# A two-layer recurrent-memory transformer block on one core: order plan iterated backward and forward, softmax over all rows from partition 0, V strips on ScalarE, V weights loaded first

## The chip, the core and the metric

One core of a Trainium2 chip runs the whole program. Its engines are TensorE (PE in the rows, PEld its weight loads), VectorE (DVE), ScalarE (ACT), GpSimd (POOL) and SyncE (SP), which here issues the transfers. The metric is the device time of one execution in microseconds (us).

## What is computed

The input x has 2048 rows of 512. Two layers follow, each with the same weights: memory-augmented recurrent attention A, then a gated FFN B.

```python
x = x + _A_ref(_layernorm(x), mem0, Wq, Wk, Wv, Wo, seg_len=32)   # 32 heads of 128
x = x + _B_ref(_layernorm(x), w_gate, w_up, w_down)               # 512 -> 1792 -> 512
x = x + _A_ref(_layernorm(x), mem0, Wq, Wk, Wv, Wo, seg_len=32)
x = x + _B_ref(_layernorm(x), w_gate, w_up, w_down)
...
for s in range(n_seg):                       # 64 segments, one after the other
    h = concatenate([mem, xs])               # 8 memory rows + 32 rows of the segment
    q, k, v = h Wq, h Wk, h Wv
    p = softmax(where(mask, q k^T * scale, -1e9))
    o = (p v) Wo
    mem = o[:, :8]; outs.append(o[:, 8:])
```

The memory of one segment is an output of the segment before it, so the 64 segments of a layer are a chain.

## The kernel before

The program runs 70 steps. Step t works on segment t of the first layer (j = 0) and segment t − 6 of the second (j = 1) at once: 40 rows each, 80 columns in one matmul. Steps 0 to 5 have the first layer alone, steps 64 to 69 the second. `hT` holds the transposed rows of a step; its memory columns come from the step before (L679, L684), and that is the recurrence.

`emit_step` goes through the 32 heads in groups of six (the last has two). For a group: Q and K matmuls (L577), casts to `qku` (L807, on ScalarE), scores (L596), the softmax on VectorE (mask add `st` L606, once for each layer; maximum L611; subtraction L613; exponential on ScalarE L616; sum L618; reciprocal L620; product `pb` L625, once for each layer), a transpose by matmul (L636), a cast to `ptsb`, probabilities times V (L649), a cast to `otsb`, and the output matmuls (L666). The first layer's scores lie in partitions 0 to 63, the second's in 64 to 103, so that one instruction can serve both where they need the same.

V rows come in two ways. The 24 last rows of each segment (`XS`) are computed by blocks of four segments (`v_pass`, L458), cast to `vst` and written to scratch memory `scr`, from which each step loads its rows into `vsb`. The memory rows and the rest change with every step: `strips` (L553) computes 32 rows for all heads, and eight casts put them into `vsb` (32 partitions x 512 each). Casts given as `("ACT", "DVE")` go to whichever engine the planner finds free; L807 is such a cast on ScalarE, L809 on VectorE.

The FFN of a block of four segments (`ffn`, L730 up and gate, L749 down, weights streamed from memory) and the V passes are background work for TensorE between the attention matmuls.

No loop sets the order on the engines. `Planner` collects tasks with an engine, an assumed duration, dependences and buffers, and `plan` makes a list schedule: a task's priority is the length of the longest chain behind it (`tail`), plus a `boost`. What it yields is emitted in that order, and each engine executes its instructions in order.

Of the kernel before, what the change touches and what calls it, by code (L numbers as in the profile page):

```python
# [10 lines left out]
F32 = mybir.dt.float32  # L11
# [63 lines left out]
class Planner:  # L75
# [48 lines left out]
    def plan(self):  # L124
# [4 lines left out]
        for bf in self.bufs:  # L129
# [118 lines left out]
class Kern:  # L248
# [48 lines left out]
    def setup_tiles(self):  # L297
# [11 lines left out]
        self.maskb = c.tile([P, L], F32, name="maskb")  # L309
        self.negh = c.tile([P, 1], F32, name="negh")  # L310
# [29 lines left out]
        self.bank = Pool([pp.tile([P, 512], F32, name=f"bank{i}") for i in range(8)], {"bg": 3, "v": 2})  # L340
        self.qkp = Pool(self.qku)
        self.vstp = Pool(self.vst)
        self.xnp = Pool(self.xn)

    def setup_consts(self):
# [15 lines left out]
        nc.vector.memset(self.negh[:], -0.5)  # L361
        for t_ in self.hT:
# [7 lines left out]
    def load_weights(self):  # L370
# [37 lines left out]
    def layernorm_T(self, xb, xkey):  # L408
# [11 lines left out]
        pl.add("ACT", act_ns(D) + 180, lambda: nc.scalar.activation(out=xn[:, :], in_=xb, func=ACTF.Identity, bias=ln[:, 10:11], scale=ln[:, 9:10]),  # L420
# [28 lines left out]
    def v_pass(self, tile, keys, pieces):  # L449

        nc, pl, DC = self.nc, self.pl, self.DC
        for k in range(self.H // 4):
# [8 lines left out]
            vs = pl.buf(self.vstp)  # L461
# [405 lines left out]
```

## Time and profile before

| | |
|---|---|
| median of 3 runs | 2171.83 us (2168.66 to 2173.26) |
| the profiled execution | 2167.7 us, its span 2165.9 us |
| granted TensorE clock, mean | 0.978 of full speed |
| busy: PE, PEld, DVE, ACT | 1890.6, 1595.0, 1521.9, 1318.9 us |
| instructions | 94004 |

Busy times are unions of the records of an engine; those of matmuls overlap, and a busy TensorE is not one at its peak. The chain that ended last is followed back from the last instruction to whatever released it.

### The profile page before, as it was taken

To read this page: it belongs to the slowest core of one execution; us is meant where nothing else is said; L and a number is where in the kernel's file an instruction comes from. 1 tells how busy PE (TensorE), PEld (TensorE's weight loads), DVE (VectorE), ACT (ScalarE), POOL (GpSimd) and SP (SyncE) were. 2 spreads that over 40 slices of the span, in tenths; PEclk is the share of its full clock that TensorE was granted. 3 is DMA by queue.
4 is the path that set the end of the run, shared out by engine and by line. 5 is a ranking of instruction groups with operands and counts; after the bars stand their busy time and mean duration, and the time that the engine had idled before them with its cause. 6 is when DMAs were issued, how large, how long until landed. Compare 5 with 4: busy or idle time off the path is not lost.

```text
span 2165.9 us, 94004 instructions
## 1 busy us (share of the span) xinstructions
PE 1890.6 (87%) x40901; PEld 1595.0 (74%) x41116; DVE 1521.9 (70%) x4377; ACT 1318.9 (61%) x2949; POOL 50.0 (2%) x93
## 2 busy tenths in 40 slices
PE   3798888989889898988989899898889899898886
PEld 2576677878777776877778787787778777777775
DVE  4475777777777775777777777767777777777664
ACT  2465666566666664666665666666665666666554
POOL 1000000000000000000000000000000000000000
PEclk8999999999999999999999999999999999999999
DMA  9314132533425245342525334252515244252633
GB/s 323 115 47 141 50 102 59 167 92 119 130 80 173 57 130 162 107 133 85 157 58 168 95 116 128 80 165 85 159 54 170 81 121 126 79 164 76 168 88 107
DMA packets 363808, 255.43 MB, mean 118 GB/s; under 512 B 21626, under 2 KB 349058, under 8 KB 363394
## 3 DMA queue, kind: packets, MB, share of 16 engines
q1 hardware_dynamic: 363394, 249.40, 38.9%
q8 instruction: 322, 5.28, 1.0%
q14 instruction: 92, 0.75, 0.1%
HBM read 222.04 MB, written 27.26 MB: 115 GB/s over the span
## 4 chain that ended last, share of the span: by engine, by line
DVE 44%; PE 36%; ACT 7%; issue 5%; DMA 4%; SPq 1%; DVEq 0%; ACTq 0%; POOLq 0%; POOL 0%
PE bank L577 13%; DVE st L606 10%; DVE pb L625 8%; PE bank L666 8%; DVE vsb L809 7%; PE bank L730 5%; DVE st L613 4%; DVE mx L611 4%; PE bank L458 4%; DVE sm L618 4%; ACT vsb L807 3%; DMA scr<-vst 2%; DVE hff L737 2%; PE bank L649 2%; PE bank L749 2%
## 5 line engine op out<-in xcount | busy, mean ns | idle before, releaser
L577 PE MATMUL bank<-hT,wq_sb 128*128 128x80 bf16 (+1 forms) x8960 | 628.2, 199 | 13.2 <-DVE hT L679 6.2
L577 PE MATMUL bank<-hT,wk_sb 128*128 128x80 bf16 (+1 forms) x8960 | 627.9, 199 | 2.9 <-issue 1.6
L807 ACT CAST qku<-bank 128x480 bf16<-128x480 f32 (+3 forms) x770 | 394.6, 514 | 192.4 <-PE bank L577 176.8
L577 PEld LDWEIGHTS <-wq_sb 128*128 128x128 bf16 x8960 | 459.1, 100 | 57.5 <-issue 47.4
L577 PEld LDWEIGHTS <-wk_sb 128*128 128x128 bf16 x8960 | 454.7, 100 | 2.7 <-DMA wk_sb<-in_A_Wk_dram 1.4
L606 DVE TENSOR_TENSOR st<-bank,maskb 64x240 f32<-64x240 f32 (+3 forms) x768 | 288.7, 376 | 216.3 <-PE bank L596 200.2
L666 PE MATMUL bank<-otsb,wo_sb 128*128 128x80 bf16 (+1 forms) x8960 | 379.1, 199 | 23.2 <-ACT otsb L807 21.7
L666 PEld LDWEIGHTS <-wo_sb 128*128 128x128 bf16 x8960 | 349.9, 100 | 44.6 <-issue 28.2
L625 DVE TENSOR_TENSOR pb<-st,rs 64x240 bf16<-64x240 f32 (+3 forms) x768 | 286.4, 373 | 17.1
L616 ACT ACTIVATE st<-st 104x240 f32<-104x240 f32 (+5 forms) x420 | 159.9, 381 | 191.8 <-DVE st L613 187.9
L807 ACT CAST otsb<-bank 128x480 bf16<-128x480 f32 (+3 forms) x420 | 200.9, 485 | 100.4 <-PE bank L649 93.6
L809 DVE CAST vsb<-bank 32x512 bf16<-32x512 f32 x262 | 180.0, 687 | 75.9 <-ACT vsb L807 71.2
L807 ACT CAST vsb<-bank 32x512 bf16<-32x512 f32 x298 | 172.0, 577 | 94.3 <-DVE vsb L809 85.2
L636 PE MATMUL bank<-ident,pb 128*128 128x80 bf16 (+1 forms) x2240 | 148.5, 200 | 79.6 <-DVE pb L625 65.7
L807 ACT CAST ptsb<-bank 128x480 bf16<-128x480 f32 (+3 forms) x348 | 169.9, 503 | 73.9 <-PE bank L636 72.4
L596 PE MATMUL bank<-qku 128*128 128x80 bf16 (+1 forms) x2240 | 169.7, 199 | 49.6 <-ACT qku L807 46.1
L636 PEld LDWEIGHTS <-pb 128*128 128x128 bf16 x2240 | 106.2, 100 | 117.5 <-DVE pb L625 92.7
L649 PE MATMUL bank<-ptsb,vsb 128*128 128x80 bf16 (+1 forms) x2240 | 147.0, 200 | 49.5 <-ACT ptsb L807 18.4
L618 DVE TENSOR_REDUCE sm<-st 104x6 f32<-104x240 f32 (+5 forms) x420 | 155.2, 369 | 44.6 <-ACT st L616 41.1
L730 PE MATMUL bank<-xnT,wg 128*128 128x128 bf16 x1792 | 179.1, 224 | 5.6 <-DVE vsb L809 1.5
L730 PE MATMUL bank<-xnT,wu 128*128 128x128 bf16 x1792 | 178.9, 224 | 3.8 <-DMA wu<-in_B_w_up_dram 3.7
L596 PEld LDWEIGHTS <-qku 128*128 128x128 bf16 x2240 | 116.4, 99 | 74.4 <-ACT qku L807 56.6
(69 smaller groups left out, 2085.0 us busy)
## 6 DMA issues: line engine op xcount, KB each, us to landing
wg<-in_B_w_gate_dram SPq DMA_DIRECT2D x224, 256.0 KB
wu<-in_B_w_up_dram SPq DMA_DIRECT2D x224, 256.0 KB
wd<-in_B_w_down_dram SPq DMA_DIRECT2D x224, 256.0 KB
vsb<-scr SPq DMA_DIRECT2D x512, 48.0 KB
scr<-vst SPq DMA_DIRECT2D x176, 96.0 KB
scr<-vst SPq DMA_DIRECT2D x144, 32.0 KB
wv_sb<-in_A_Wv_dram SPq DMA_DIRECT2D x4, 1024.0 KB
wq_sb<-in_A_Wq_dram SPq DMA_DIRECT2D x5, 768.0 KB
```

Source lines behind the costliest of these rows:

```text
L577: nc.tensor.matmul(o_ap, lhsT=W[:, c, h * P:(h + 1) * P], rhs=mv(c), start=(c == 0), stop=(c == DC - 1))
L596: nc.tensor.matmul(s_all(SB)[:, uh - h0 + i, :], lhsT=qku[:, i, 0, :], rhs=fview(qku[:, i, 1, q0:q0 + 1], qc), start=True, stop=True)
L606: pl.add("DVE", dve_ns(n, True), lambda gsz=gsz, hs=hs, st=st, SB=SB, pj_=pj_, npj_=npj_, idx=idx: nc.vector.tensor_tensor(out=st[pj_, hs] ...
L616: pl.add("ACT", act_ns(n), lambda hs=hs, st=st: nc.scalar.activation(out=st[pr, hs], in_=st[pr, hs], func=ACTF.Exp, scale=self.scale), r=s ...
L618: pl.add("DVE", dve_ns(n), lambda hs=hs, st=st, sm=sm: nc.vector.tensor_reduce(out=sm[pr, hs], in_=st[pr, hs], axis=AX.X, op=ALU.add), r=s ...
L625: pl.add("DVE", dve_ns(n), lambda gsz=gsz, hs=hs, st=st, rs=rs, pb=pb, pj_=pj_, npj_=npj_, kc=kc: nc.vector.tensor_tensor(out=pb[pj_, hs, ...
L636: nc.tensor.matmul(o_ap, lhsT=pb[:, hl, :], rhs=idn, start=True, stop=True)
L649: nc.tensor.matmul(OB[:, hl * ncol:(hl + 1) * ncol], lhsT=self.vsb[:, h * P:(h + 1) * P], rhs=ptsb[:, hl, 0:ncol], start=True, stop=True)
L666: nc.tensor.matmul(WB[:, c * ncol:(c + 1) * ncol], lhsT=self.wo[:, h, c * P:(c + 1) * P], rhs=otsb[:, hl, 0:ncol], start=(h == 0 and c == ...
L730: nc.tensor.matmul(gu[:, 2 * i + k, :], lhsT=W[:, c, i * P:(i + 1) * P], rhs=xnT[:, c, :], start=(c == 0), stop=(c == DC - 1))
L807: nc.scalar.copy(out=dst, in_=src)
L809: nc.vector.tensor_copy(out=dst, in_=src)
```

## The change

Five things. (1) `plan` makes ten rounds: a forward list schedule, then a backward one over the reversed dependences whose finishing times become the new priorities, and so on; the round with the shortest planned span is kept. The assumed durations of VectorE and ScalarE instructions are changed too. (2) Instructions of the softmax start at partition 0: the mask add of the second layer goes over all 104 rows first, and that of the first layer then overwrites rows 0 to 63; the product `pb` is done for each layer over all rows, with a column of the 0/1 tile `jm` as a scalar, which zeroes the rows of the other layer. (3) The eight strip casts are ScalarE's. (4) At the start all V weights load ahead of the others (`boot`), the first six V passes have nine buffers in place of three (six of them halves of the FFN weight tiles `wd`), and their writes to `scr` are issued by ScalarE. (5) V passes may hold three of the eight PSUM banks in place of two.

```diff
 def dve_ns(n, psum=False):
-    return n / 0.96 + (42.0 if psum else 70.0)
+    return n / 0.96 + (74.0 if psum else 67.0)
 def act_ns(n, psum=False):
-    return n * 0.833 + (75.0 if psum else 120.0)
+    return n * 0.833 + (52.0 if psum else 110.0)
...
+        for k in range(rounds):
+            if k:
+                self.backward()
+            order = self.forward()
+            self.spans.append(self.span)
+            if best is None or self.span < best[0]:
+                best = (self.span, order, [tk.start for tk in order], [tk.on for tk in order], [bf.slot for bf in self.bufs])
...
+    def backward(self):
...
+                tk = T[heapq.heappop(h)[1]]
+                fin = now + tk.dur
+                free[e] = fin
+                tk.tail = fin + tk.boost
...
-        self.bank = Pool([pp.tile([P, 512], F32, name=f"bank{i}") for i in range(8)], {"bg": 3, "v": 2})
+        self.bank = Pool([pp.tile([P, 512], F32, name=f"bank{i}") for i in range(8)], {"bg": 3, "v": 3})
...
+        self.bootp = Pool(self.vst + [w[:, k, :] for w in self.wd for k in range(2)])
...
+        nc.vector.memset(self.jm[:], 0.0)
+        nc.vector.memset(self.jm[0:JOFF, 0:1], 1.0)
+        nc.vector.memset(self.jm[JOFF:P, 1:2], 1.0)
...
+    def boot(self):
+
+        self.nboot = getattr(self, "nboot", 0) + 1
+        return 1e7 - 1e4 * self.nboot
...
-                pl.add("SP", 430, lambda vs=vs, d=d, c0=c0, n=n: nc.sync.dma_start(out=d, in_=vs[c0:c0 + BLK * n, :]),
-                       r=[vs], w=[("vd", j, b, q, k) for q in range(r0 // 8, (r0 + n) // 8)])
+                pl.add("ACT" if boot else "SP", 430, lambda vs=vs, d=d, c0=c0, n=n, q=nc.scalar if boot else nc.sync: (
+                    q.dma_start(out=d, in_=vs[c0:c0 + BLK * n, :]), None)[1], lat=2200.0 + 2000.0 * boot,
...
             for k in range(8):
-                pl.add(("ACT", "DVE"), act_ns(512, True), lambda k=k: (
+                pl.add("ACT", act_ns(512, True), lambda k=k: (
                     self.vsb[32:64, k * 512:(k + 1) * 512], vb[k // 4][32 * (k % 4):32 * (k % 4) + 32, :]), r=[vb[k // 4]], w=[("vs", k)])
...
-            for idx, j in enumerate(jobs):
-                pj_ = slice(0, JOFF) if j == 0 else slice(JOFF, LW)
+            for idx, j in reversed(list(enumerate(jobs))):
+                pj_ = slice(JOFF if not both and j else 0, JOFF if j == 0 else LW)
...
-                    out=pb[pj_, hs, kc:kc + L], in0=st[pj_, hs],
+                    out=pb[pr, hs, kc:kc + L], in0=st[pr, hs], scalar=self.jm[pr, j:j + 1],
+                    in1=rs[pr, hs].unsqueeze(2).to_broadcast([npart, gsz, L]), op0=ALU.mult, op1=ALU.mult),
...
         p0 = self.pre1(0)
+        p1 = self.pre1(1)
         self.load_weights()
-        p1 = self.pre1(1)
-        self.v_group([0, 1, 2, 3], {0: p0, 1: p1})
-        self.v_group([4, 5, 7, 8], {})
+        self.v_group([0, 1, 2, 3], {0: p0, 1: p1}, True)
+        self.v_group([4, 5, 7, 8], {}, True)
```

How the order moves is seen at three places. The first is VectorE in step 54, behind its first head group; the tiles are numbered by buffer, `st_81` and `st_82` being two head groups in turn. Before:

```order
L618 TENSOR_REDUCE sm_88<-st_82 104x6
L611 TENSOR_REDUCE mx_85<-st_81 104x6
L620 RECIPROCAL rs_90<-sm_88 104x6
L613 TENSOR_TENSOR st_81<-st_81,mx_85 104x240
L625 TENSOR_TENSOR pb_84<-st_82,rs_90 64x6x40
L625 TENSOR_TENSOR pb_84<-st_82,rs_90 40x6x40
L618 TENSOR_REDUCE sm_87<-st_81 104x6
L620 RECIPROCAL rs_89<-sm_87 104x6
L809 CAST vsb<-bank_144 32x512 x2
L809 CAST vsb<-bank_141 32x512 x2
L606 TENSOR_TENSOR st_82<-bank_138,maskb 64x240
L606 TENSOR_TENSOR st_82<-bank_138,maskb 40x240
```

and in the changed kernel, where the lines are L677 (mask add), L682, L684, L689, L691 and L694 (`pb`), and the two groups are `st_82` and `st_83`:

```order
L689 TENSOR_REDUCE sm_88<-st_82 104x6
L677 TENSOR_TENSOR st_83<-bank_139,maskb 104x240
L691 RECIPROCAL rs_90<-sm_88 104x6
L677 TENSOR_TENSOR st_83<-bank_139,maskb 64x240
L694 SCALAR_TENSOR_TENSOR pb_84<-st_82,jm,rs_90 104x6x40
L682 TENSOR_REDUCE mx_87<-st_83 104x6
L694 SCALAR_TENSOR_TENSOR pb_84<-st_82,jm,rs_90 104x6x40
L684 TENSOR_TENSOR st_83<-st_83,mx_87 104x240
L677 TENSOR_TENSOR st_82<-bank_144,maskb 104x240
L677 TENSOR_TENSOR st_82<-bank_144,maskb 64x240
L689 TENSOR_REDUCE sm_89<-st_83 104x6
```

The four strip casts are gone, and the instructions of one head group now stand between those of the other.

The second is ScalarE in the middle of a step of the steady phase. Before:

```order
L616 ACTIVATE st_82<-st_82 104x240
L616 ACTIVATE st_81<-st_81 104x240
L807 CAST vsb<-bank_141 32x512 x2
L807 CAST qku_78<-bank_145 128x12x40
L807 CAST vsb<-bank_143 32x512
L807 CAST qku_79<-bank_142 128x12x40
L807 CAST ptsb_91<-bank_138 128x480
L807 CAST ptsb_92<-bank_140 128x480
L807 CAST qku_77<-bank_145 128x8x40
L807 CAST otsb_94<-bank_142 128x480
L807 CAST vsb<-bank_143 32x512
```

and in the changed kernel (L877 is the cast, L687 the exponential):

```order
L687 ACTIVATE st_83<-st_83 104x240
L687 ACTIVATE st_82<-st_82 104x240
L877 CAST vsb<-bank_139 32x512 x3
L877 CAST qku_80<-bank_143 128x12x40
L877 CAST vsb<-bank_139 32x512
L877 CAST vsb<-bank_140 32x512
L877 CAST ptsb_93<-bank_142 128x480
L687 ACTIVATE st_83<-st_83 104x240
L877 CAST qku_78<-bank_145 128x8x40
L877 CAST vsb<-bank_140 32x512
L877 CAST ptsb_94<-bank_143 128x480
L877 CAST otsb_95<-bank_142 128x480
```

Six of the step's eight strip casts stand in these rows (four of them before), behind nearly all `qku` casts; one `ptsb` cast stands where two stood.

The third is the start, on SP's queue. Before:

```order
L378 DMA wq_sb<-in_A_Wq_dram 128x4x768
L378 DMA wk_sb<-in_A_Wk_dram 128x4x768
L378 DMA wq_sb<-in_A_Wq_dram 128x4x768
L378 DMA wk_sb<-in_A_Wk_dram 128x4x768
L358 DMA maskb<-st_81 40x40
L378 DMA wv_sb<-in_A_Wv_dram 128x4x1024
L378 DMA wq_sb<-in_A_Wq_dram 128x4x768
L378 DMA wk_sb<-in_A_Wk_dram 128x4x768
L378 DMA wv_sb<-in_A_Wv_dram 128x4x1024 x3
L378 DMA wq_sb<-in_A_Wq_dram 128x4x768
L378 DMA wk_sb<-in_A_Wk_dram 128x4x768
```

and in the changed kernel (L443 the weights, L561 the input rows for a V pass, whose tile must have been read by ScalarE before it is loaded again):

```order
L443 DMA wv_sb<-in_A_Wv_dram 128x4x1024
L561 DMA xo_105<-in_A_x_dram 128x512
L420 DMA maskb<-st_82 40x40
L443 DMA wv_sb<-in_A_Wv_dram 128x4x1024 x2
L561 DMA xp_115<-in_A_x_dram 128x512
L561 DMA xo_105<-in_A_x_dram 128x512
L443 DMA wv_sb<-in_A_Wv_dram 128x4x1024
L443 DMA wq_sb<-in_A_Wq_dram 128x4x768
L561 DMA xp_115<-in_A_x_dram 128x512
L443 DMA wk_sb<-in_A_Wk_dram 128x4x768
L443 DMA wo_sb<-in_A_Wo_dram 128x6x512
L443 DMA wq_sb<-in_A_Wq_dram 128x4x768
```

The V weights stand ahead of Q, K and output weights, and input loads stand between them.

## Rows read from the trace of the kernel before

**Rows 1.** Page part 4: the chain that ended last, by engine and by line.

```profile
...
DVE 44%; PE 36%; ACT 7%; issue 5%; DMA 4%; SPq 1%; DVEq 0%; ACTq 0%; POOLq 0%; POOL 0%
PE bank L577 13%; DVE st L606 10%; DVE pb L625 8%; PE bank L666 8%; DVE vsb L809 7%; PE bank L730 5%; DVE st L613 4%; DVE mx L611 4%; PE bank L458 4%; DVE sm L618 4%; ACT vsb L807 3%; DMA scr<-vst 2%; DVE hff L737 2%; PE bank L649 2%; PE bank L749 2%
...
```

**Rows 2.** Windows, by phase: us, busy PE, PEld, DVE, ACT, POOL, clock, DMA, GB/s.

```profile
...
0.00:76.20 76.20, 35.48 (x578) 23.56 (x585) 31.02 (x89) 22.41 (x50) 9.40 (x20) 0.82 0.80 265
76.20:243.00 166.80, 147.61 (x3387) 114.36 (x3410) 107.94 (x333) 100.89 (x254) 4.74 (x8) 0.97 0.33 95
243.00:1969.60 1726.60, 1544.56 (x32803) 1319.96 (x32974) 1258.45 (x3598) 1087.62 (x2366) 33.61 (x61) 0.99 0.39 114
1969.60:2165.90 196.30, 162.91 (x4133) 137.13 (x4147) 124.53 (x359) 107.98 (x281) 2.20 (x4) 0.97 0.40 116
...
```

**Rows 3.** Windows, four steps, cut where VectorE writes the next memory rows.

```profile
...
997.74:1025.45 27.71, 25.11 (x582) 22.56 (x584) 20.80 (x58) 18.10 (x40) 0.21 (x1) 1.00 0.28 81
1025.45:1052.87 27.42, 25.19 (x576) 22.13 (x576) 21.30 (x64) 18.04 (x40) 0.55 (x1) 1.00 0.45 130
1052.87:1087.99 35.12, 31.64 (x645) 28.10 (x650) 23.73 (x70) 21.31 (x49) 0.55 (x1) 0.95 0.66 194
1087.99:1119.32 31.33, 27.68 (x547) 21.73 (x549) 23.10 (x67) 19.69 (x40) 0.79 (x2) 1.00 0.18 53
...
```

**Rows 4.** Chain in order of time, second of these steps: start, us, what.

```profile
...
1025.41 0.89 PE bank L730 x16
...
1028.13 0.86 PE bank L577 x24
...
1029.14 0.40 DVE st L606
...
1048.72 0.43 DVE hff L737
...
```

**Rows 5.** The same view in the fourth of these steps.

```profile
...
1094.88 1.73 PE bank L458 x8
...
```

**Rows 6.** Waits, whole span: us in total, times, longest us.

```profile
...
ACT vsb L807 <- DVE vsb L809: 85.2, 102, 1.6
...
```

**Rows 7.** Timeline of TensorE, third step; in brackets the idle time before.

```profile
...
1074.25 0.28 PE L596 MATMUL bank<-qku 128*128 128x80 bf16 x3 [2.08 <-ACT qku L807]
...
```

**Rows 8.** Windows, in the third step.

```profile
...
1076.00:1080.00 4.00, 3.95 (x59) 3.53 (x59) 3.60 (x11) 3.08 (x8) 0.00 (x0) 0.75 0.52 151
...
```

**Rows 9.** Groups by line and shape: busy us, mean ns, idle before.

```profile
...
L809 DVE CAST vsb<-bank 32x512 bf16<-32x512 f32 x262 | 180.0, 687 | 75.9 <-ACT vsb L807 71.2
...
L807 ACT CAST vsb<-bank 32x512 bf16<-32x512 f32 x298 | 172.0, 577 | 94.3 <-DVE vsb L809 85.2 <-PE bank L553 5.0
...
L606 DVE TENSOR_TENSOR st<-bank,maskb 40x240 f32<-40x240 f32 x320 | 131.4, 411 | 21.0 <-PE bank L596 13.9
...
L606 DVE TENSOR_TENSOR st<-bank,maskb 64x240 f32<-64x240 f32 x320 | 127.5, 398 | 190.9 <-PE bank L596 184.9
...
L737 DVE SCALAR_TENSOR_TENSOR hff<-th,bank 128x256 bf16<-128x256 f32 x224 | 93.4, 418 | 59.3 <-ACT th L735 56.0
...
L809 DVE CAST ptsb<-bank 128x480 bf16<-128x480 f32 x28 | 18.3, 653 | 0.9 <-PE bank L636 0.5
...
```

**Rows 10.** Timeline of VectorE, first of the four steps: start, us, what.

```profile
...
1005.19 0.40 DVE L625 TENSOR_TENSOR pb<-st,rs 40x240 bf16<-40x240 f32 x1
...
1005.62 0.40 DVE L611 TENSOR_REDUCE mx<-st 104x6 f32<-104x240 f32 x1
...
1006.93 0.41 DVE L613 TENSOR_TENSOR st<-st,mx 104x240 f32<-104x240 f32 x1
1007.25 0.40 DVE L611 TENSOR_REDUCE mx<-st 104x6 f32<-104x240 f32 x1
...
```

**Rows 11.** Timeline near the end of step 0, TensorE and SP's queue.

```profile
...
44.91 0.99 SPq L465 DMA_DIRECT2D scr<-vst  x2
...
54.01 0.36 PE L649 MATMUL bank<-ptsb,vsb 128*128 128x40 bf16 x6 [6.75 <-DMA vsb<-scr]
...
```

More of the change, by code (lines that the diff above doesn't have):

```diff
@@ L140, in plan, with forward @@
             tk.tail = m + tk.dur + tk.boost
+        best = None
+        self.spans = []
+        for k in range(rounds):
[5 more added lines that the diff above has]
+                best = (self.span, order, [tk.start for tk in order], [tk.on for tk in order], [bf.slot for bf in self.bufs])
+        self.span, order, starts, ons, slots = best
+        for tk, st, on in zip(order, starts, ons):
+            tk.start, tk.on = st, on
+        for bf, sl in zip(self.bufs, slots):
+            bf.slot = sl
+        return order
+    def backward(self):
+        T = self.tasks
+        left = [len(tk.succ) for tk in T]
+        rdy = [0.0] * len(T)
+        free, heaps, events = {}, {}, []
+        end = [tk.start + tk.dur for tk in T]
+        for tk in T:
+            free.setdefault(tk.on, 0.0)
+            heaps.setdefault(tk.on, [])
+            if left[tk.idx] == 0:
+                heapq.heappush(events, (0.0, tk.idx))
+        n, now = len(T), 0.0
+        while n:
+            while events and events[0][0] <= now:
+                i = heapq.heappop(events)[1]
+                if i >= 0:
+                    heapq.heappush(heaps[T[i].on], (-end[i], i))
+            did = False
+            for e, h in heaps.items():
+                if free[e] > now or not h:
+                    continue
+                tk = T[heapq.heappop(h)[1]]
+                fin = now + tk.dur
+                free[e] = fin
+                tk.tail = fin + tk.boost
+                heapq.heappush(events, (fin, -1))
+                n -= 1
+                did = True
+                for d in tk.deps:
+                    rdy[d] = max(rdy[d], fin + self.gap(T[d], tk))
+                    left[d] -= 1
+                    if left[d] == 0:
+                        heapq.heappush(events, (rdy[d], d))
+            if not did and n:
+                now = max(now, events[0][0])
+    def forward(self):
+        T = self.tasks
+        for bf in self.bufs:
+            bf.first, bf.left, bf.slot, bf.t_free = None, len(set(bf.users)), None, 0.0
+            bf.pool.free = [(0.0, None, i) for i in range(len(bf.pool.tiles))]
+            bf.pool.used = {}
         free = {"PE": 0.0, "ACT": 0.0, "DVE": 0.0, "POOL": 0.0, "SP": 0.0}
@@ L375, in load_weights, with ld @@
         wo_v = self.Wo.rearrange("h e d -> e h d")
-        def ld(name, dst, src, nb, keys):
-            pl.add("SP", nb / 300.0, lambda: nc.sync.dma_start(out=dst, in_=src), w=keys, boost=1e6)
+        def ld(dst, src, ns, keys):
+            pl.add("SP", ns, lambda: nc.sync.dma_start(out=dst, in_=src), w=keys, boost=self.boot())
         for h0 in range(0, self.H, 8):
             cs = slice(h0 * P, (h0 + 8) * P)
-            ld("wv", self.wv[:, :, cs], wv_v[:, :, cs], P * self.DC * 8 * P * 2, [("wv", h) for h in range(h0, h0 + 8)])
-        for (h0, gsz, us) in self.groups:
+            ld(self.wv[:, :, cs], wv_v[:, :, cs], P * self.DC * 8 * P * 2 / 300.0, [("wv", h) for h in range(h0, h0 + 8)])
+        for g, (h0, gsz, us) in enumerate(self.groups):
             cs = slice(h0 * P, (h0 + gsz) * P)
@@ L392, in load_mem0 @@
         m0 = self.xo[0][0:MEM, :]
-        pl.add("SP", 100, lambda: nc.sync.dma_start(out=m0, in_=self.mem0), w=[("xo", 0)], boost=2e6)
+        pl.add("SP", 100, lambda: nc.sync.dma_start(out=m0, in_=self.mem0), w=[("xo", 0)], boost=self.boot())
         B = pl.buf(self.bank, "bg")
@@ L482, in v_group, with ln_x @@
                     xi = (base + q) % 2
-                    self.v_pass(self.xvf[xi], [("xvf", xi, g) for g in range(4)], pcs[q])
+                    self.v_pass(self.xvf[xi], [("xvf", xi, g) for g in range(4)], pcs[q], boot)
                     pcs[q] = []
-    def ln_x(self, b):
+    def ln_x(self, b, boot=False):
         nc, pl = self.nc, self.pl
@@ L496, in pre1 @@
         xb = self.xs[i]
-        pl.add("SP", 430, lambda: nc.sync.dma_start(out=xb[:], in_=self.x_in[b * P:(b + 1) * P, :]), w=[("xs", i)], boost=(2e6 if b < 2 else 0))
+        pl.add("SP", 430, lambda: nc.sync.dma_start(out=xb[:], in_=self.x_in[b * P:(b + 1) * P, :]), w=[("xs", i)], boost=(self.boot() if b < 2 else 0))
         self.xw[(0, b)] = i
```

36 lines of the change are left out of this document (18 added, 18 removed).

## The prediction

> **What bounds the kernel now.** I read the chain of waits first. VectorE holds 44% of the span on it and TensorE 36%; by line, the VectorE casts `vsb` (L809) alone are 7%, beside the softmax lines L606, L625, L613, L611 and L618 [rows 1]. So neither engine is the bound all the time: something inside a step alternates. The windows by phase show where to look [rows 2]: the 56 steps with both layers run from 243.0 to 1969.6 us, 30.8 us a step, TensorE busy 1545 of 1727 us, VectorE 1258, ScalarE 1088. What lies in front (243 us) and behind (196 us) is a fifth.
>
> Four steps in a row repeat through the steady phase: 27.7, 27.4, 35.1 and 31.3 us [rows 3]. In the second of them the chain is plain [rows 4]: TensorE work leads up to the first score bank, from 1029.14 on the chain lies on VectorE, one softmax instruction behind the other, until 1048.72, and then it is TensorE's again until the next step. That is 3.7 us of head, 19.6 us of VectorE, 4 us of tail. A step is short or long by the FFN and V work that TensorE has on top.
>
> What must TensorE do at least? Issue distances come from bursts in the chain: 24 matmuls of 80 columns in 0.86 us (36 ns), 16 of 128 columns in 0.89 us (56 ns) [rows 4], 8 of 512 columns in 1.73 us (216 ns) [rows 5]. A round of four steps has 1920 of the first kind (69 us), 240 of the second (FFN up and gate, transposes: 13 us), 60 of the third (V and FFN down: 13 us) and the strips, 128 that go four side by side (7 us): 102 us, where the four steps take 121.6. With the extra V group at block 4 (96 matmuls of 512 columns) the mean is 25.9 us a step against 30.8 measured. TensorE thus loses 4.9 us a step, though its records overlap and look 89% busy.
>
> The long step shows how it is lost. The `vsb` casts are handed to and fro between VectorE and ScalarE, each waiting for the other's (102 such waits on ScalarE's side, 85 us in all); here the `qku` cast behind them is late, TensorE stands 2.08 us until 1074.25, and from 1076 to 1080 its granted clock is 0.75 of full speed, so half of that at the lower level, 1.2 GHz [rows 6 to 8]. That is one stall paid twice.
>
> **The change, part by part**, for the 56 steady steps. Counts are from the order of instructions, prices from rows.
>
> Strips on ScalarE: 212 `vsb` casts leave VectorE at 0.687 us, −146 us, and come to ScalarE at 0.577 us, +122 us [rows 9]. ScalarE is busy 63% of this phase, and the new plan gives 123 wide `ptsb` casts to VectorE in return (0.653 us each, +80 us [rows 9]; some 30 small copies add 8). So VectorE's net is −58 us, and ScalarE goes from 1088 us to about 1088 + 122 − 71 = 1139, with the `ptsb` casts taken at the 0.577 us of its nearest row: it has room on average. The mutual waits between the two engines on `vsb` end, since one engine writes them in order.
>
> All rows from partition 0: the mask add of the second layer covers 104 rows where it covered 40. The time does not follow rows: 64 rows take 398 ns, 40 rows 411 [rows 9], so 0, bounded by 13 ns × 336 = ±4 us. The `pb` product becomes a three-operand instruction with a per-row 0/1 scalar, over 104 rows twice. No such shape is in the trace; the nearest is `hff`, the same operation, 418 ns for 256 elements, against 0.40 us of today's `pb` for 240 [rows 9, 10]. I take 0; plus or minus 20 ns on 672 of them is ±13 us.
>
> What that does to the seams between instructions is worth more. A `pb` on rows 64 to 103 ends at 1005.59 and the independent L611 on all rows starts at 1005.62, a gap of 0.03 us; L613 starts at 1006.93, lasts 0.41, and the independent L611 after it starts at 1007.25, 0.09 us before the end [rows 10]. So a change of starting partition, or of a dependence, costs about 0.11 us against a pair that starts at the same partition. The Trainium skill (VectorE: DVE Perf Modes, section on two Vector instructions with no wait between them) says the same in a rule: an instruction whose start quadrant differs from the last one's is held until all earlier ones have finished. These rows agree. In the steady steps 1424 of 3598 seams change the starting partition; after the change none does. Some of them become dependences (the two mask adds now overlap in rows, so the second waits for the first), but the new order weaves two head groups together, and independent seams at one partition go from 1614 to 2885. At 0.11 us that is −140 us.
>
> VectorE's stream: −146 + 88 − 140 = −198 us, 3.5 us a step. If all of it came off the path, a step would take 27.3 us. TensorE needs 25.9 and cannot overlap all of its head and tail, and short and long steps each meet their own limit: those with 24 us of matmuls would be held by VectorE at about 24 + 1, the one with 30 by TensorE at 32 to 33. I take 28.3 us, one above the path's figure: −2.5 us × 56 = −140 us.
>
> V weights first, boot: today the first step ends at 76.2 us with TensorE busy 35 us [rows 2], and TensorE waits 6.75 us there for V rows to come back through memory [rows 11]. The six boot V passes (192 matmuls of 512 columns, 41 us) are spread so that 176 V matmuls lie in steps 1 to 6; after the change 192 lie before the end of step 0 and 32 in steps 1 to 6. That takes 31 us of TensorE from 166.8 us in which it is busy 148, and starts the first FFN a step earlier. I take −25 us. Step 0 itself must now fit 41 us of V and some 14 of its own behind the first weights; its `wk` and `wo` loads stand behind input loads that wait for ScalarE, and ScalarE now issues 96 transfers. What an issue costs ScalarE no row shows; on SP's queue one takes 0.5 us [rows 11], so the bounds are 0 and 48 us, beside other ScalarE work in a phase where it is busy 22 of 76 us. I take +5 for step 0: −20 together, from −40 to +20.
>
> The last 196 us: single-layer steps start at partition 64 throughout, so only the strips move; seven steps, about 1 us each: −6 us.
>
> Third PSUM bank for V, planner costs, iteration: they move instructions, and that is in the counts above; no price of their own.
>
> **Sum.** 2167.7 us (the profiled execution; its span is 2165.9) − 140 − 20 − 6 = 2002 us. The profiled execution is 4 us under the median of 2171.83, so against that median it is 2006, and the times below are given that way too.
>
> **Rivals.**
> *The seams stay.* The new order makes two adds dependent, and nearly every instruction names a semaphore of its own engine. The skill's section on the drain (same page, "The DRAIN you can't avoid") says that the next operation does not start before the pipe is empty, whatever the semaphores; by it the seam term is 0. The 0.09 us overlap in [rows 10] speaks against that. Then VectorE gives 58 us, 1 us a step, on the path with the mutual waits: 2172 − 56 − 26 = 2090. Chance 0.12.
> *All of the path is gained.* TensorE follows wherever VectorE lets it: 27.3 us a step, −197, boot and end −26: 1949. For it: in heads and tails TensorE is already full. Against: 27.3 is only 1.4 above its floor in the mean, and the floor is uneven. Chance 0.12.
> *Boot eats its gain*: ScalarE stuck in 96 issues while `qku` casts of step 0 wait behind them, +25 in place of −20: 2051. Chance 0.05.
> *Slower: ScalarE's run of strips.* Up to five `vsb` casts stand in a row there, 2.9 us, with a `qku` cast behind. If TensorE runs dry behind that in each step as it does today in the long one, it costs 2.1 us of standing and about as much at the lower clock, 4 us: 56 × (4 − 2.5) = +84, less 26: 2230. It decides from 3 us a step. Against it: in the new order all but one or two `qku` casts are ahead of the run. Chance 0.05.
> The forecast has 0.66, and its own range is 1965 to 2055.
>
> **Numbers.** The likeliest is 2006. To leave out no more than 2 in 10, the range takes in most of the first two rivals: 1940 to 2095. A difference of 0.2% (4 us) is about what can be told from none. All cases but the last are faster; for a mixture of half-gains that cancel I leave 0.02: faster 0.93, same 0.02, slower 0.05.
>
> **What would show it.** Right: VectorE's `vsb` rows gone and ScalarE's at 560; in steady windows VectorE busy some 160 us less at nearly the same sum of durations; steps of about 25, 25.5, 32.5 and 27 us; the waits of `vsb` on `vsb` gone; TensorE's clock near 1.00 in the long step; step 0 ending near 80 us and step 6 near 223. Wrong: a `pb` above 0.43 us, seams still 0.03 us apart, `qku` casts late behind `vsb` on ScalarE with TensorE standing and a clock of 0.75 in every step, or a step 0 that ends past 95 us.

## The result and the profile after

The changed kernel takes 2012.77 us (median of 4 runs, 2010.93 to 2013.82) against 2170.61 for the kernel before, run beside it: ratio 0.9271, 95% interval 0.9255 to 0.9287. Forecast were 2006 and a range of 1940 to 2095. The profiled execution has a span of 2009.1 us.

The page's chain, by engine and by line, answers to [rows 1]:

```profile
PE 60%; DVE 14%; ACT 13%; DMA 8%; issue 3%; SPq 1%; ACTq 0%; POOL 0%; DVEq 0%; POOLq 0%
PE bank L648 24%; PE bank L736 10%; PE bank L800 7%; ACT vsb L877 5%; PE bank L528 5%; PE bank L624 4%; PE bank L819 3%; DVE pb L694 3%; DVE st L677 3%; DMA scr<-vst 3%; PE bank L667 3%; ACT otsb L877 3%; PE bank L719 2%; PE bank L706 2%; DVE sm L689 1%
```

VectorE was 44% of the chain and is 14%; TensorE went from 36 to 60%. The windows, cut at the same four events as [rows 2] (end of step 0, of step 6, of step 62, of the program), with the same columns:

```profile
0.00:116.77 116.77, 72.12 (x740) 37.88 (x741) 58.41 (x142) 25.52 (x57) 11.05 (x23) 0.87 0.69 219
116.77:249.24 132.47, 119.35 (x3254) 102.16 (x3254) 87.85 (x297) 93.30 (x230) 2.75 (x5) 0.92 0.27 79
249.24:1824.91 1575.67, 1508.32 (x32974) 1304.11 (x32974) 1118.60 (x3541) 1140.19 (x2423) 33.73 (x61) 1.00 0.43 125
1824.91:2009.10 184.19, 161.30 (x4152) 135.32 (x4149) 116.16 (x352) 117.56 (x288) 2.46 (x4) 0.97 0.42 123
```

The 56 steady steps give 150.9 us (28.1 us a step; forecast 28.3), the end 12.1. The start loses: step 0 ends 40.6 us later, steps 1 to 6 are 34.3 us shorter, together +6.2 where −20 was forecast. Four steps at the same place of the round of four as in [rows 3] (steps 35 to 38 here, 31 to 34 there):

```profile
1056.94:1081.44 24.50, 23.21 (x572) 21.56 (x572) 17.99 (x59) 18.30 (x38) 0.55 (x1) 1.00 0.28 81
1081.44:1108.84 27.40, 26.69 (x594) 23.16 (x592) 20.29 (x65) 19.62 (x42) 0.55 (x1) 1.00 0.47 134
1108.84:1139.94 31.10, 30.60 (x651) 26.59 (x649) 21.43 (x69) 22.29 (x50) 1.10 (x2) 1.00 0.75 220
1139.94:1168.04 28.10, 26.19 (x552) 21.43 (x550) 21.77 (x70) 22.01 (x45) 1.10 (x2) 1.00 0.21 60
```

24.5, 27.4, 31.1 and 28.1 us, and the granted clock is 1.00 in the long step too (0.95 in [rows 3]). Inside the first of them the chain, in order of time, is no longer 20 us of VectorE as in [rows 4]:

```profile
1057.22 2.74 PE bank L648 x72
...
1067.06 1.84 PE bank L624 x32
1068.90 0.55 PE bank L800 x8
...
1071.49 0.59 ACT vsb L877
1072.09 0.43 ACT qku L877
...
1074.63 0.58 ACT vsb L877
...
1078.20 0.42 DVE hff L807
1078.62 0.44 DVE pb L694 x2
...
1079.35 0.86 PE bank L736 x24
```

TensorE leads for 14 us; then the strip casts on ScalarE alternate with what stands behind them; after the memory write that opens the step, VectorE appears only at 1078. [Rows 4] shows the second step of its round; in the second one here TensorE leads the chain for the first 17 us. Groups by line and shape, as in [rows 9]:

```profile
L877 ACT CAST vsb<-bank 32x512 bf16<-32x512 f32 x560 | 323.5, 578 | 20.2 <-PE bank L624 6.2 <-PE bank L528 1.3
L694 DVE SCALAR_TENSOR_TENSOR pb<-st,jm,rs 104x240 bf16<-104x240 f32 x580 | 250.4, 458 | 4.6 <-PE bank L706 3.3
L677 DVE TENSOR_TENSOR st<-bank,maskb 104x240 f32<-104x240 f32 x290 | 116.7, 402 | 192.2 <-PE bank L667 183.1 <-ACT st L687 0.6 <-PE bank L648 0.5
L879 DVE CAST ptsb<-bank 128x480 bf16<-128x480 f32 x156 | 100.3, 643 | 8.1 <-PE bank L706 7.5
L807 DVE SCALAR_TENSOR_TENSOR hff<-th,bank 128x256 bf16<-128x256 f32 x224 | 91.4, 412 | 81.9 <-ACT th L805 80.5
```

All 560 strip casts are ScalarE's, and the waits of `vsb` on `vsb` [rows 6] are gone. `pb` takes 458 ns, not 400.

### The profile page after: what moved, and what is told of

It reads as the page before. It is cut to its first block, busy times and chain, and to the rows that moved or that the text cites. A ratio compares the mean times of both kernels' runs of the same rounds, so it can differ in the third digit from the quotient of the medians.

```text
span 2009.1 us, 94214 instructions
## 1 busy us (share of the span) xinstructions
PE 1861.1 (93%) x41116; PEld 1579.5 (79%) x41116; DVE 1381.0 (69%) x4331; ACT 1376.6 (69%) x2998; POOL 50.0 (2%) x93
## 4 chain that ended last, share of the span: by engine, by line
PE 60%; DVE 14%; ACT 13%; DMA 8%; issue 3%; SPq 1%; ACTq 0%; POOL 0%; DVEq 0%; POOLq 0%
PE bank L648 24%; PE bank L736 10%; PE bank L800 7%; ACT vsb L877 5%; PE bank L528 5%; PE bank L624 4%; PE bank L819 3%; DVE pb L694 3%; DVE st L677 3%; DMA scr<-vst 3%; PE bank L667 3%; ACT otsb L877 3%; PE bank L719 2%; PE bank L706 2%; DVE sm L689 1%
## 5 line engine op out<-in xcount | busy, mean ns | idle before, releaser
L877 ACT CAST qku<-bank 128x480 bf16<-128x480 f32 (+3 forms) x770 | 394.2, 513 | 257.9 <-PE bank L648 204.6
L677 DVE TENSOR_TENSOR st<-bank,maskb 64x240 f32<-64x240 f32 (+5 forms) x768 | 284.8, 371 | 243.1 <-PE bank L667 224.5
L877 ACT CAST vsb<-bank 32x512 bf16<-32x512 f32 x560 | 323.5, 578 | 20.2 <-PE bank L624 6.2
L694 DVE SCALAR_TENSOR_TENSOR pb<-st,jm,rs 104x240 bf16<-104x240 f32 (+4 forms) x768 | 311.3, 431 | 8.2 <-PE bank L706 4.1
L877 ACT CAST otsb<-bank 128x480 bf16<-128x480 f32 (+3 forms) x420 | 201.8, 486 | 47.7 <-PE bank L719 33.5
L687 ACT ACTIVATE st<-st 104x240 f32<-104x240 f32 (+5 forms) x420 | 160.2, 382 | 87.4 <-DVE st L684 69.6
L689 DVE TENSOR_REDUCE sm<-st 104x6 f32<-104x240 f32 (+5 forms) x420 | 153.5, 366 | 71.5 <-ACT st L687 70.0
L667 PE MATMUL bank<-qku 128*128 128x80 bf16 (+1 forms) x2240 | 169.6, 198 | 25.5 <-ACT qku L877 24.0
L800 PE MATMUL bank<-xnT,wu 128*128 128x128 bf16 x1792 | 174.2, 220 | 4.4 <-DMA wu<-in_B_w_up_dram 4.2
L800 PE MATMUL bank<-xnT,wg 128*128 128x128 bf16 x1792 | 174.9, 220 | 2.5 <-ACT xnT L877 1.1
L684 DVE TENSOR_TENSOR st<-st,mx 104x240 f32<-104x240 f32 (+5 forms) x420 | 156.4, 373 | 4.6
L682 DVE TENSOR_REDUCE mx<-st 104x6 f32<-104x240 f32 (+5 forms) x420 | 153.5, 366 | 4.3
L719 PEld LDWEIGHTS <-vsb 128*128 128x128 bf16 x2240 | 111.3, 99 | 46.9 <-issue 18.2
```

The costliest lines, as they stand in the source:

```text
L667: nc.tensor.matmul(s_all(SB)[:, uh - h0 + i, :], lhsT=qku[:, i, 0, :], rhs=fview(qku[:, i, 1, q0:q0 + 1], qc), start=True, stop=True)
L677: pl.add("DVE", dve_ns(n, True), lambda gsz=gsz, hs=hs, st=st, SB=SB, pj_=pj_, npj_=npj_, idx=idx: nc.vector.tensor_tensor(out=st[pj_, hs] ...
L684: pl.add("DVE", dve_ns(n), lambda gsz=gsz, hs=hs, st=st, mx=mx: nc.vector.tensor_tensor(out=st[pr, hs], in0=st[pr, hs], in1=mx[pr, hs].uns ...
L687: pl.add("ACT", act_ns(n), lambda hs=hs, st=st: nc.scalar.activation(out=st[pr, hs], in_=st[pr, hs], func=ACTF.Exp, scale=self.scale), r=s ...
L689: pl.add("DVE", dve_ns(n), lambda hs=hs, st=st, sm=sm: nc.vector.tensor_reduce(out=sm[pr, hs], in_=st[pr, hs], axis=AX.X, op=ALU.add), r=s ...
L694: pl.add("DVE", dve_ns(n), lambda gsz=gsz, hs=hs, st=st, rs=rs, pb=pb, j=j, kc=kc: nc.vector.scalar_tensor_tensor(out=pb[pr, hs, kc:kc + L ...
```

## The experiments

"Steady" is the 56 steps, cut in each trace where VectorE writes the next memory rows; VectorE's busy time is that of the same window. Windows are of the profiled execution, which lies up to 5 us from the median. Medians are of four runs, beside the kernel before (2170.6 to 2171.8 us). Each kernel was planned anew and so has an order of its own, except d1, d2 and f1, which keep that of b3, of the changed kernel and of e2.

| kernel | median us | ratio (95%) | step 0, step 6 end | steady us | VectorE busy there |
|---|---|---|---|---|---|
| before | 2171 | 1 | 76.2, 243.0 | 1726.6 | 1258 |
| b1_plan_only | 2103.0 | 0.9689 (0.9674–0.9703) | 77.3, 239.9 | 1671.8 | 1236 |
| b2_strips_only | 2042.7 | 0.9413 (0.9397–0.9428) | 76.8, 238.0 | 1614.1 | 1145 |
| b3_rows_only | 2074.8 | 0.9556 (0.9542–0.9570) | 76.2, 241.7 | 1630.4 | 1161 |
| c1_strips_rows | 2031.0 | 0.9351 (0.9335–0.9367) | 76.0, 237.4 | 1606.8 | 1108 |
| d1_b3_order_old_rows | 2145.5 | 0.9882 (0.9868–0.9897) | 76.7, 242.7 | 1702.9 | 1232 |
| d2_after_order_old_rows | 2052.8 | 0.9453 (0.9436–0.9470) | 117.7, 250.3 | 1616.6 | 1170 |
| e3_one_round | 2073.1 | 0.9555 (0.9540–0.9569) | 120.5, 257.6 | 1624.8 | 1083 |
| e4_strips_both | 2093.1 | 0.9649 (0.9633–0.9666) | 117.9, 253.0 | 1644.4 | 1204 |
| e5_rows_apart | 2029.3 | 0.9349 (0.9335–0.9363) | 115.7, 247.5 | 1594.3 | 1165 |
| changed kernel | 2012.8 | 0.9271 (0.9255–0.9287) | 116.8, 249.2 | 1575.7 | 1119 |
| e1_old_boot | 2000.1 | 0.9208 (0.9184–0.9233) | 77.6, 240.2 | 1574.5 | 1118 |
| e2_boot_pool | 1992.7 | 0.9182 (0.9165–0.9199) | 99.2, 229.4 | 1580.9 | 1119 |
| f1_pb_first_two_operand | 1983.0 | 0.9135 (0.9120–0.9149) | 97.3, 227.7 | 1566.8 | 1099 |

### One part taken back from the changed kernel

**The start (e1_old_boot).** `load_weights`, `v_pass`, `v_group` and their callers as before: load order, three buffers, writes to `scr` on SP.

```diff
-        self.v_group([0, 1, 2, 3], {0: p0, 1: p1}, True)
+        self.v_group([0, 1, 2, 3], {0: p0, 1: p1})
...
-            vs = pl.buf(self.bootp if boot else self.vstp)
+            vs = pl.buf(self.vstp)
```

> The changed kernel with the start of before: Q and K weights first, three buffers for the V passes, their writes issued by SP. Theory A (the start eats its gain: ScalarE stands in the transfers that it issues, so step 0 ends at 117 us in place of 76, and that cancels the V work taken out of steps 1 to 6): step 0 ends near 76, step 6 near 228, the steady steps stay at 28.1 us, the time is about 1992 us (1985 to 2000). Rival B (V work in steps 1 to 6 costs what step 0 saves): step 6 ends near 249 again and the time is 2008 to 2018.

2000.1 us, by 12.7 less than the changed kernel: the new start costs time, as theory A has it, though the median lies a hair above its 1985 to 2000 and the four runs spread from 1991 to 2003. Step 0 is back at 77.6; step 6 ends at 240.2, not 228.

**The iteration (e3_one_round).**

```diff
-    def plan(self, rounds=10):
+    def plan(self, rounds=1):
```

> The changed kernel with one forward schedule only, no iteration. Theory A (the gain is VectorE's shorter stream, by strips and seams): within 25 us of the changed kernel, 2013 to 2038, steady steps below 28.7 us. Rival C (the iterated order is what gains): most of it is lost, 2080 to 2150, steady steps above 29.3 us.

2073.1: between the two theories, and far from nothing. By the medians one round costs 60 us; between the profiled executions it is 66, of which 49 are steady, with VectorE busy less than in the changed kernel (1083 against 1119 us, with 3468 instructions against 3541). The waits from 250 to 1750 us name the place; the row of the changed kernel first, then that of one round (us in total, times, longest):

```profile
DVE st L677 <- PE bank L667: 168.7, 90, 3.9
```

```profile
DVE st L677 <- PE bank L667: 238.7, 90, 4.2
```

With one round, VectorE waits 70 us more for score banks. The ten rounds also divide the casts and copies in another way: with one round 73 fewer instructions of the steady steps are VectorE's, and 74 more are ScalarE's. What of the 49 us is order and what is this division was not tried apart.

**The strips (e4_strips_both).**

```diff
-                pl.add("ACT", act_ns(512, True), lambda k=k: (
+                pl.add(("ACT", "DVE"), act_ns(512, True), lambda k=k: (
```

> The changed kernel with the strip casts free for either engine again. Theory A (mutual waits of the vsb casts and their 0.69 us on VectorE's stretch cost about 1.5 us a step): 2070 to 2110 us, vsb waits on vsb back at over 50 us in all. Rival D (TensorE is the bound now and hides it, the plan puts ptsb on ScalarE in return): 2010 to 2030.

2093.1, as theory A has it: 80 us, 69 of them steady. The mutual waits are back in its list of waits:

```profile
ACT vsb L877 <- DVE vsb L879: 82.1, 87, 2.4
DVE vsb L879 <- ACT vsb L877: 23.5, 43, 5.9
```

**The softmax rows (e5_rows_apart).** Mask add and `pb` of before, planned anew.

> The changed kernel with the softmax of before: mask add and pb on rows 0 to 63 and 64 to 103 apart. Theory A (seams that change the starting partition are 0.03 us apart in place of overlapping by 0.08, worth 140 us of VectorE's stream; the dearer pb, 0.458 us in place of 0.405, gives 35 us back; TensorE hides about half): 2050 to 2100 us. Rival E (no seam effect, only the cheaper pb): 1985 to 2013 us.

2029.3: only 16.5 us, outside what either theory expected. But the planner made another order for it, so this run alone says nothing of the seams. d2 below holds the order.

### One part alone put into the kernel before

> The kernel before with the iterated plan and the new assumed durations alone (strip casts on both engines, softmax rows and the start as before). One round in place of ten cost the changed kernel 60 us, 49 of them in the 56 steady steps, where the prediction had given the plan no price of its own. Theory A: the order has a worth of its own, whatever the instructions are; VectorE still bounds the step, so about the same is had here: 2095 to 2125 us, steady steps about 30.0 us. Rival C: the iteration pays only where VectorE has been relieved, since with it as the bound no order shortens its stream: 2150 to 2175 us. Rival F: the order is worth more where VectorE is the bound, since it lets two head groups overlap: 2050 to 2090 us.

> The kernel before with the eight strip casts given to ScalarE alone (one-round plan, old durations, softmax rows and start as before). Giving them back cost the changed kernel 80 us. Theory A: the strips are worth VectorE's relief in either kernel, since VectorE is the bound here even more: 2080 to 2110 us, no waits of vsb on vsb, VectorE busy 100 to 150 us less. Rival G: without the iterated plan the casts stand in a run on ScalarE with qku casts behind them, and the gain is lost again: 2140 to 2180 us.

> The kernel before with the softmax of the change alone: mask adds and pb over all rows from partition 0 (one-round plan, strips on both engines, start as before). In the changed kernel this part was worth 16 us net, with TensorE then the bound. Theory A: the seams are worth about 0.1 us each on VectorE, but pb takes 55 ns more (672 of them, 37 us), and the old order makes fewer neighbours independent; VectorE is the bound here, so what its stream gains shows in full: 2110 to 2145 us. Rival E: seams gain little without the woven order and the longer pb takes it: 2160 to 2200 us.

2103.0, 2042.7 and 2074.8. The plan has a worth of its own, as theory A has it; strips and rows give 37 and 35 us more than the best end of theory A, and their rivals are out. The three gains, 69, 129 and 97 us, add to 295; together with the start the change gave 158. In the steady steps of these two a us off VectorE's busy time goes with about a us off the steps: b2 has 114 us less busy and is 112 shorter, b3 98 and 96.

**Two of them (c1_strips_rows).** The softmax rows of b3 and the strip line of b2 together.

> The kernel before with strips on ScalarE and softmax rows from partition 0 together (one-round plan, old durations, start as before). Alone they gave 129 and 97 us; the changed kernel with one round but the new durations and the new start stood at 2073 us with 29.0 us in a steady step, no better than the strips alone (28.8). Theory A: the two relieve the same engine, and from about 28.5 us a step TensorE's floor and the order bound it, so together they give little more than the strips: 2015 to 2045 us. Rival N: the new assumed durations make a poor one-round order, and without them both gains add up more: 1985 to 2010 us. Rival W: rows from partition 0 with the added dependence hurt once the strips are gone: 2045 to 2080 us.

2031.0, theory A: 12 us beyond the strips alone, though VectorE is busy another 37 us less. It stands below e3's 2073, which has the new durations, the new start and the third bank besides; which of those spoils a one-round order in the steady steps (18 us) was not tried apart.

### The same order, other instructions

d1 and d2 leave each engine's order as it is in b3 and in the changed kernel and put back the old rows and operands:

```diff
-                pj_ = slice(JOFF if not both and j else 0, JOFF if j == 0 else LW)
+                pj_ = slice(JOFF if j else 0, JOFF if j == 0 else LW)
...
-                    out=pb[pr, hs, kc:kc + L], in0=st[pr, hs], scalar=self.jm[pr, j:j + 1],
-                    in1=rs[pr, hs].unsqueeze(2).to_broadcast([npart, gsz, L]), op0=ALU.mult, op1=ALU.mult),
+                    out=pb[pj_, hs, kc:kc + L], in0=st[pj_, hs],
+                    in1=rs[pj_, hs].unsqueeze(2).to_broadcast([npj_, gsz, L]), op=ALU.mult),
```

> The order of b3 on every engine, instruction for instruction, but each mask add and pb with the rows and the operands that it had before (starts at partition 64 for the second layer, two-operand pb). So only the instructions differ from b3 (2074.8 us), and only the order, made under one more dependence, from before (2171.8 us). Theory A: b3 gained by its seams: without them 2135 to 2170 us. Rival O: b3 gained because the added dependence happened to give the list schedule a better order; the seams are worth no more than pb's extra 55 ns take back: 2065 to 2100 us.

> The changed kernel's order on every engine, instruction for instruction, with the old rows and operands of mask add and pb. Theory A: the seams are worth what the prediction said on VectorE's stream (1424 seams at 0.1 us, less 672 times 55 ns for pb, about 105 us), and TensorE hides half or more of it: 2040 to 2080 us, steady VectorE waits and TensorE's idle time both up. Rival O: in this order seams at partition 64 cost next to nothing, because VectorE waits for others there anyway: 2005 to 2030 us, like the kernel with the softmax of before.

2145.5 and 2052.8: theory A both times. The instructions are worth 71 us in b3 and 40 in the changed kernel; the other 26 of b3's 97 came by its order. The timelines of VectorE show the seam at the same three instructions, first in d2:

```profile
1114.51 0.40 DVE L689 TENSOR_REDUCE sm<-st 104x6 f32<-104x240 f32 x1
1114.95 0.41 DVE L677 TENSOR_TENSOR st<-bank,maskb 40x240 f32<-40x240 f32 x1
1115.39 0.19 DVE L691 RECIPROCAL rs<-sm 104x6 f32<-104x6 f32 x1
```

then in the changed kernel:

```profile
1090.71 0.40 DVE L689 TENSOR_REDUCE sm<-st 104x6 f32<-104x240 f32 x1
1091.03 0.40 DVE L677 TENSOR_TENSOR st<-bank,maskb 104x240 f32<-104x240 f32 x1
1091.35 0.18 DVE L691 RECIPROCAL rs<-sm 104x6 f32<-104x6 f32 x1
```

The add on rows 64 to 103 starts 0.04 us after the sum has ended, that on all rows 0.08 us before it ends; the reciprocal behind it starts 0.03 after and 0.08 before the add's end. 0.88 us from the first start to the third are 0.64. Over the whole trace the median of such pairs is a gap of 0.03 us in d2 and an overlap of 0.08 in the changed kernel (42 pairs with this add behind the sum, 50 with the reciprocal behind the add). Pairs that start at partition 0 in both, as the add on rows 0 to 63 and a sum behind it, overlap by 0.075 in both. So the starting partition makes the difference, and not the order.

### The start again, and a faster version

**Writes on GpSimd's queue (e2_boot_pool).**

```diff
-                pl.add("ACT" if boot else "SP", 430, lambda vs=vs, d=d, c0=c0, n=n, q=nc.scalar if boot else nc.sync: (
+                pl.add("POOL" if boot else "SP", 430, lambda vs=vs, d=d, c0=c0, n=n, q=nc.gpsimd if boot else nc.sync: (
```

> The changed kernel with its start left as it is, except that the 96 writes of V rows to scratch at the start are issued by GpSimd's queue in place of ScalarE's. Theory A: step 0 ends at 117 us because ScalarE stands in its own issues, each waiting in line for a tile or a weight, with casts behind: step 0 then ends at 80 to 95 us and the whole takes 1980 to 1998 us. Rival B: the start is late because the weight and input loads stand in SP's queue in that order (V weights ahead of Q and K, input loads that wait for ScalarE between them): step 0 still ends at 108 to 118 us, the whole 2005 to 2015 us.

1992.7, theory A on the total; step 0 ends at 99.2, short of its 95 but 17.6 earlier, and step 6 at 229.4. What stood in the way is in the changed kernel's timeline of ScalarE (ACTq is its queue of transfers):

```profile
77.75 0.40 ACT L687 ACTIVATE st<-st 64x240 f32<-64x240 f32 x1 [4.65 <-DMA scr<-vst]
77.78 0.60 ACTq L536 DMA_DIRECT2D scr<-wd  x1
79.38 1.12 ACTq L536 DMA_DIRECT2D scr<-vst  x2
83.38 4.07 ACTq L536 DMA_DIRECT2D scr<-wd  x6
88.35 1.14 ACTq L536 DMA_DIRECT2D scr<-vst  x2
89.53 0.53 ACTq L536 DMA_DIRECT2D scr<-wd  x1
90.31 1.23 ACTq L536 DMA_DIRECT2D scr<-vst  x2
91.77 1.96 ACTq L536 DMA_DIRECT2D scr<-wd  x2
93.78 0.36 ACT L877 CAST qku<-bank 128x240 bf16<-128x240 f32 x1 [15.62 <-DMA vsb<-scr]
```

and in that of TensorE:

```profile
94.19 0.28 PE L667 MATMUL bank<-qku 128*128 128x40 bf16 x3 [8.52 <-ACT qku L877]
```

For 15.6 us ScalarE executes nothing but 16 issues, of 0.5 to 0.6 us each, and stands between them; a `qku` cast is behind them, and TensorE stands 8.5 us for it. The 96 issues take 50 us by themselves (median 0.53); their rows, in which issues close to each other are joined with the waits between, add up to 67. The issuing is the smaller part of the delay. Of the chain in step 0 it has 4.7% (ACTq), while transfers that must land have most of it. `scr` are the writes of V rows, out of `vst` or the halves of `wd`; the second row, from the same chain in order of time, is a write for which the issue at 83.38 stood:

```profile
by line: DMA scr<-vst 21.0%; DMA scr<-wd 16.6%; DMA wk_sb<-in_A_Wk_dram 10.8%; DMA wo_sb<-in_A_Wo_dram 7.1%; DMA wg<-in_B_w_gate_dram 5.0%; ACTq L536 4.7%; PE bank L528 4.6%; DMA xo<-in_A_x_dram 4.1%; DVE ident L412 3.4%; issue 2.2%; PE ban
...
76.09 7.22 DMA scr<-vst
```

The weight loads (L443) on SP are held too. SP's list of waits, from the start to 120 us, has them wait for writes that ScalarE issued, though these touch other tiles; why, no run shows:

```profile
SPq L443 <- DMA scr<-wd: 14.7, 7, 3.1
SPq L443 <- DMA scr<-vst: 12.8, 4, 5.4
```

With GpSimd as the issuer there are no such waits, and the last of the Q, K and output weights is issued at 68.2 us in place of 84.1:

```profile
84.06 0.37 SPq L443 DMA_DIRECT2D wo_sb<-in_A_Wo_dram  x1
```

```profile
68.19 2.06 SPq L443 DMA_DIRECT2D wo_sb<-in_A_Wo_dram  x1
```

In e2's own chain of step 0 the weight loads are gone, and the writes of V rows have 44%:

```profile
by line: DMA scr<-wd 31.8%; DMA scr<-vst 12.5%; PE bank L528 12.4%; POOL scr L536 6.5%; issue 5.7%; PE bank L736 4.4%; DVE ident L412 4.1%; PE bank L648 2.2%; PE bank L499 1.7%; ACT xn L490 1.7%; DVE hT L428 1.4%; DVE lns L484 1.2%; ACT vst
```

Casts of the V passes wait there for a buffer whose write must land, as this one in ScalarE's timeline:

```profile
64.59 0.59 ACT L877 CAST wd<-bank 128x512 bf16<-128x512 f32 x1 [1.05 <-DMA scr<-wd]
```

The plan for e2 also moved about 30 instructions of step 0 from VectorE to ScalarE. So the 20 us are those of the queue and of this order together; the queue in the changed kernel's own order was not tried.

**The first layer's `pb` with two operands (f1_pb_first_two_operand)**, on top of e2, rows 0 to 63, still from partition 0:

```diff
+                    out=pb[0:JOFF, hs, kc:kc + L], in0=st[0:JOFF, hs],
+                    in1=rs[0:JOFF, hs].unsqueeze(2).to_broadcast([JOFF, gsz, L]), op=ALU.mult) if j == 0 else nc.vector.scalar_tensor_tensor(
```

> The changed kernel with the boot writes on GpSimd's queue (1992.7 us), and the first layer's pb made a two-operand product over rows 0 to 63 again; it starts at partition 0 like all others, and the second layer's pb stays as changed. Same order. 336 instructions in the steady steps at about 55 ns less: VectorE's busy time 18 us less there, no new seams. Theory A: on the path in part: 1980 to 1990 us. Rival T: TensorE is the bound now and hides it: 1990 to 1996 us.

1983.0, theory A: 9.7 us less than e2 by the medians. Between the profiled executions, of which e2's lies 4.7 us above its median, the steady steps are 14 us shorter, with VectorE busy 21 us less there. It is the fastest of all kernels here, 1.5% below the changed one. Its `pb` groups:

```profile
L696 DVE SCALAR_TENSOR_TENSOR pb<-st,jm,rs 104x240 bf16<-104x240 f32 x290 | 131.3, 453 | 0.0
L694 DVE TENSOR_TENSOR pb<-st,rs 64x240 bf16<-64x240 f32 x320 | 125.8, 393 | 5.7 <-PE bank L708 4.2
```

## Why the prediction was right

The total was 7 us off, by a sum whose terms were off by more. That it came so near is in part luck: the start was 26 us worse than forecast, the steady steps and the end together 17 better.

**What bounds it, and the mutual waits: right.** The chain moved to TensorE, steps came to 28.1 us (forecast 28.3), near 24.5, 27.4, 31.1 and 28.1 where 25, 25.5, 32.5 and 27 stood; the clock is 1.00 in the long step; with strips on both engines again the 106 us of mutual waits and 80 us of time come back.

**VectorE's stream: right in kind and size, with one wrong price.** The −198 counts the short gaps at the seams; the busy time leaves them out, and for it the prediction named some 160 us. Measured are 140 us of busy time in the steady steps, and the gaps of up to 50 ns between VectorE's instructions, summed over the traces, fell from 59 to 16 us. Together that is −183. The durations alone fell by 33, so the seams gave about 150, where 140 was forecast. d2, the new order with old rows, divides this: it has 65 us less of durations than the kernel before (casts and `ptsb` were put at −146 + 88 = −58) and 40 us from its seams. The new instructions add the other 110 us of seams and cost 32 us of durations. In those 32, `pb` is the loss: 560 times 59 ns and 112 times 61 (its wide and narrow rows against d2's), 40 us. The step that failed is the price of `pb`, taken as 0 and bounded by ±13 us: the neighbour chosen, `hff`, did not tell it, at 412 to 418 ns for 256 elements against 458 for 240. The prediction had named a `pb` above 0.43 us as a sign of being wrong, and it came.

**From stream to step: held by an offset.** The forecast let 140 of 198 us reach the end, a rate of 0.7. Where the order is held the rate is lower or alike: of the 77 us between d2 and the changed kernel, gaps counted, 41 reach the steps (0.5), of the 103 between d1 and b3, 73 (0.7), and of f1's 21, 14 (0.7; by the medians 10). At 0.5 the 183 us of VectorE would be some 97, at 0.7 some 128, both estimates from these runs; 151 were found. The rest fits the iteration.

**Iteration and durations "no price of their own": wrong.** One round in place of ten costs 49 us in the steady steps and 60 in all, and in the kernel before the plan with the new durations alone gives 55 and 69. What it saves is waiting, 70 us of it for score banks, while VectorE is given more casts. The counts of instructions and seams, on which the forecast rested, can't see a wait. A term of this size was missing, and it made up for what TensorE hid of VectorE's gain.

**Boot, −20: wrong.** +6 was measured, and the sign that the prediction named for it, a step 0 past 95 us, is there. Steps 1 to 6 gave 34 (forecast 25). Step 0 took 40.6 more in place of 5. The bounds of 0 and 48 us held the issues alone, which take 50. What they left out is that an issue stands until an earlier transfer has landed, with ScalarE's casts behind it, and that the weight loads stand behind the same writes: transfers that must land have most of step 0's chain. That is near to the rival "Boot eats its gain", ScalarE stuck in its issues, which was given 0.05 and would have cost 25. Off ScalarE, and in the order planned for that, 20 us come back, 17.6 of them in step 0. Step 0 still ends at 99 and not near 80: by e2's chain the writes of V rows hold it, and TensorE is busy 69 us of it (35 before), since the boot V passes now lie there.

**The end, −6:** −12; b2, strips alone, has 188.8 us there against 196.3, so the other part comes with the rest.

**Rivals.** "The seams stay" (2090) fell with the rows above. The Trainium skill (VectorE: DVE Perf Modes, section on two Vector instructions with no wait between them) holds an instruction back whose starting quadrant differs from the last one's; d2 against the changed kernel agrees, 0.04 us behind against 0.08 ahead. The Trainium skill's section on the drain (same page), by which the prediction had 0 for the seams here, adds that a next operation that is not held starts earlier, so it gave no reason for a 0. "All of the path" (1949) fell: TensorE now has 60% of the chain, and VectorE's gain reached the steps in part only. "ScalarE's run of strips" was not seen: the chain holds strip casts from 1071 to 1078, but at a clock of 1.00, and the strips alone, with the old one-round plan, gave 129 us.

Not tried: the third PSUM bank, and the new durations apart from the iteration.

## What to carry to other kernels

Price a planner's rounds as a term of their own: a count of instructions shows what an engine must do, not how long it waits. Compare a forecast with the measure that it was made in: a busy time leaves out the short gaps that a stream counts. To learn what an instruction is worth, hold the order and change the instruction; a new plan turned 40 us into 16, and gains of 69, 129 and 97 us that each stood alone came to 158 together, as the chain moved from VectorE to TensorE. And before a queue is chosen for transfers, ask what each issue may have to wait for, and what that engine has to execute behind it.

## What was not expected of the hardware

A `pb` with a per-row scalar, 104x240 float32 in SBUF, takes 458 ns where the two-operand form takes 392 on 64 rows and 405 on 40; `hff`, the same operation with one operand in PSUM, takes 412 for 256 elements. The number of rows is not the reason: in the single-layer steps the form with the scalar takes 453 ns on 64 rows and 467 on 40. What else it is was not tried.

An issue takes ScalarE 0.5 us (median of 96), like one on SP's queue (0.5, [rows 11]), and on GpSimd's it takes about as long (4 in 2.47 us). The Trainium skill (DMA: Bandwidth & Descriptors, section on issuing engines not being separate DMA queues) says that issuing from several engines saves only the sequencer's time, usually small beside the transfer. Here the 96 issues take 50 us of ScalarE's time in step 0, and the run with another issuer, in its own order, is 20 us shorter.
